# The opening loads of a gated attention and feed-forward kernel: 256-KB second halves, and the Q weights on a second queue

## The chip, the core and the metric

The kernel runs on one core of a Trainium2 chip. A core has five engines that run side by side: TensorE (PE, matrix products, with PEld its weight loads), VectorE (DVE), ScalarE (ACT), GpSimd (POOL) and SyncE (SP). Data come from memory by DMA. A DMA is issued by an instruction on one of the engines' own streams, here SyncE's or ScalarE's, and the transfers of both streams are carried by the same 16 DMA engines. A semaphore tells the waiting engine that a load has landed. The metric is device time in microseconds (us), as the median of several runs.

## What is computed

Cut to what matters, with x of 2048 tokens by 512 in bfloat16:

```python
g = sigmoid((x * gate_w).sum(-1, keepdims=True))
q, k, v = x @ wq, x @ wk, x @ wv            # 32 heads of 16, 4 segments of 512 tokens
for s in range(4):                           # per head
    p = softmax(qs @ ks.T / 4 + causal_mask)
    a_dot = p @ vs
    a_mem = (phi(qs) @ M) / (phi(qs) @ z + 1e-6)
    o_s = sigmoid(beta) * a_mem + (1 - sigmoid(beta)) * a_dot
    M, z = M + phi(ks).T @ vs, z + phi(ks).sum()
a = concat(o_s) @ wo
b = (gelu(x @ w_gate) * (x @ w_up)) @ w_down # inner width 1792
out = g * a + (1 - g) * b
```

## The kernel before

All of the program is a set of named tasks, each a few instructions on one engine. The order in which every engine works through its tasks is written out by hand in the table `ORDER`, one list for each engine, and the streams are emitted in that order. A planner in the file (`Sched`) only merges the five lists into one sequence by estimated times, from which waits between engines are derived; the estimates (`est`, `issue`, the byte counts given to a load) don't reach the chip.

The four segments of 512 tokens are worked through one after the other, each with projections K, Q and V, attention, gate and up products and the down product, interleaved on TensorE. The change lies in the first 10 us or so, the opening.

In the opening, the first segment of x (512 tokens by 512, 512 KB) is loaded in four pieces `x0_0` to `x0_3` of 128 tokens (128 KB each) into `xin`, which is the first part of the buffer `hT[1]`. Pieces 0 and 1 are its first half, pieces 2 and 3 its second. TensorE turns them with 16 transposes (line 596, tasks `x0t0_0`, `x0t1_0` for the first half, `x0t0_1`, `x0t1_1` for the second) into PSUM, and four copies (line 604, tasks `x0ev0_0` to `x0ev1_1`, all on VectorE before) bring the result to `xT[0]`: `x0ev0_1` brings the first 256 input features of the second half's tokens, `x0ev1_1` the other 256. The K weights `wk` come in four blocks of 128 input rows, `w_wk0` to `w_wk3`, of 128 KB each. Before these loads land, seven matmuls on constants keep TensorE busy (line 588, `warm0` to `warm6`).

TensorE's order in the opening is: six `warm` matmuls, transposes of the first half, `warm6`, eight K matmuls on the first half with the first two blocks of `wk`, transposes of the second half, the remaining K matmuls (three of them come later), then Q (blocks 0 and 1 of `wq` are one load, blocks 2 and 3 the other), then V with `wv`. K matmuls in the opening take 256 tokens each, so a name such as `K0_1.6` is segment 0, output tile 1, instruction 6: second half of the tokens, input block 2. Matmuls of all projections carry line 498, copies from PSUM lines 512 (ScalarE) and 515 (VectorE).

All loads are issued by `dma` (line 529; the transposing loads of the later x segments at line 525). SyncE issues, in this order: `x0_0`, `w_wk0`, `x0_2`, `w_wk2`, both halves of `wq`, both halves of `wv` (256 KB each), the first half of the gate weights `wg` (896 KB), the four transposing loads of the second segment of x with the gate vector `gwb` and `beta` between them, and the second half of `wg`. ScalarE issues `x0_1`, `w_wk1`, `x0_3` and `w_wk3`; then it loads the table for exp (`tload`, line 560) and next copies from PSUM.

Of the kernel before, what the change touches and what calls it, by code (L numbers as in the profile page):

```python
# [7 lines left out]
PE, ACT, DVE, POOL, SP = "pe", "act", "dve", "pool", "sp"  # L8
# [13 lines left out]
P = 128  # L22
# [62 lines left out]
        "D3_3w0.4 D3_2.8 D3_2.10 D3_2.12 D3_2.14 D3_3w1.0 D3_3w1.4 D3_3w1.8 D3_0.16 D3_1.14 D3_3w1.12 D3_3a1.0 "  # L85
        "D3_2.16 D3_3w0.8 D3_1.16 D3_3w0.12 D3_3a0.0 "),
    "act": (
        "x0_1 w_wk1 x0_3 w_wk3 tload K0_0even pke0_0 Q0_2ev Q0_1ev Q0_3ev kl0_20 Q0_0ev Vev0_1 K0_3ev exp0_0A0 "
        "gsum0_0 Gev0_6 exp0_0B0 pke0_1 gexp exp0_0L gsum0_3 Gev1_7 exp0_0A1 Q1_0ev exp0_0B1 pqe1_0 gexs0 "
        "exp0_1A0 Gev1_10 Gev1_2 exp0_1B0 pqe1_1 exp0_1A1 K1_0ev Gev0_11 exp0_1B1 gsum1_1 K1_3ev exp0_2A0 Gev1_4 "  # L90
        "exp0_2B0 gsum1_3 Gev0_2 exp0_2L Gev0_7 gexs1 exp0_2A1 Gev1_9 exp0_2B1 Vev1_2 exp0_3A0 Q2_2ev Vev1_3 "
        "exp0_3B0 Gev1_13 Gev0_13 exp0_3A1 Vev1_0 Gev1_1 exp0_3B1 gelu0_0 gelu0_2 Q2_0ev gelu0_6 gelu0_10 "
        "gelu1_0 gelu1_7 exp1_0A0 pke1_0 exp1_0B0 exp1_0L pke1_1 exp1_0A1 fin0_2 exp1_0B1 pqe2_0 exp1_1A0 fin0_0 "
        "exp1_1B0 pqe2_1 exp1_1A1 exp1_1B1 exp1_2A0 exp1_2B0 fin0_3 exp1_2L Vev2_0 exp1_2A1 gsum2_1 exp1_2B1 "
        "exp1_3A0 Q3_0ev exp1_3B0 gexs2 exp1_3A1 Q3_1ev exp1_3B1 gelu2_0 gelu2_1 gelu2_2 gelu2_3 gelu2_4 gelu2_5 "
        "gelu2_6 gelu2_7 gelu2_8 gelu2_9 gelu2_10 gelu2_11 gelu2_12 gelu2_13 exp2_0A0 pke2_0 exp2_0B0 pke2_1 "
        "exp2_0L Q3_3ev Vev3_0 exp2_0A1 exp2_0B1 pqe3_0 exp2_1A0 exp2_1B0 pqe3_1 exp2_1A1 exp2_1B1 K3_0ev "
        "exp2_2A0 exp2_2B0 exp2_2L exp2_2A1 exp2_2B1 exp2_3A0 gsum3_2 exp2_3B0 exp2_3A1 K3_3ev exp2_3B1 gexs3 "
        "gelu3_0 gelu3_1 gelu3_2 gelu3_3 gelu3_4 gelu3_5 gelu3_6 gelu3_7 gelu3_8 gelu3_9 gelu3_10 gelu3_11 "
        "gelu3_12 gelu3_13 exp3_0A0 exp3_0B0 exp3_0L exp3_0A1 fin2_0 exp3_0B1 exp3_1A0 exp3_1B0 exp3_1A1 "  # L100
        "exp3_1B1 exp3_2A0 exp3_2B0 exp3_2L exp3_2A1 exp3_2B1 exp3_3A0 exp3_3B0 exp3_3A1 exp3_3B1 fin3_0 fin3_1 "
        "fin3_30 "),
    "dve": (
        "x0ev0_0 x0ev1_0 x0ev0_1 x0ev1_1 K0_1ev kl0_11 K0_0ev kp0_1 kl0_01 kl0_10 K0_2ev kp0_2 kl0_21 gmul0 "
        "kp0_0 kl0_00 Vev0_0 pkc0_0 Vev0_2 kp0_3 Gev0_1 Q1_2ev Gev1_5 Gev0_4 kl0_30 kl0_31 Vev0_3 pkc0_1 Q1_3ev "
        "gsum0_2 Gev1_11 Q1_1ev gsum0_1 Gev0_8 K1_2ev pqc1_0 Gev1_3 gmat Gev0_5 mzacc0 pvt0_0_0 pvt0_0_1 pqc1_1 "
        "gmul1 Gev1_12 K1_1ev gsum1_0 Gev0_12 Gev0_10 GdT0 Vev1_1 norm0_0 pvt0_1_0 pvt0_1_1 mzbd0 Gev0_9 gsum1_2 "
        "Gev1_6 gts1 Gev1_8 nump1_00 Gev0_3 nump1_01 nump1_02 norm0_1 Q2_1ev pvt0_2_0 pvt0_2_1 kp1_0 nump1_11 "
        "norm0_2 Gev0_0 pvt0_3_0 nump1_10 Q2_3ev Gev1_0 pvt0_3_1 Um0_0 Um0_1 norm0_3 Um0_2 Um0_9 Um0_7 Um0_8 "
        "Um0_12 Um0_4 Um0_6 Um1_2 Um0_3 Um1_3 Um1_5 Um0_5 kl1_00 Um0_13 kl1_01 Um0_11 nump1_12 kp1_1 Um0_10 "  # L110
# [17 lines left out]
        "msk2_3B1 msk2_3A0 msk2_3B0 exsT3 msk3_0B0 msk3_0A0 msk3_0L msk3_0A1 msk3_0B1 msk3_1A1 msk3_1B1 msk3_1A0 "  # L128
        "msk3_1B0 msk3_2B0 msk3_2L msk3_2A1 msk3_2A0 msk3_2B1 msk3_3A0 msk3_3B0 msk3_3A1 msk3_3B1 "),
    "sp": (  # L130
        "x0_0 w_wk0 x0_2 w_wk2 w_wq0 w_wq1 w_wv0 w_wv1 w_wg0 x1_0 w_gwb x1_1 w_beta x1_2 x1_3 w_wg1 pkT0_1 "
        "Vlo0_0 Vlo0_1 pkT0_2 pkT0_0 pkT0_3 xt1 x2_3 x2_2 x2_1 x2_0 w_wu0 oTd1_1 oTd1_0 w_wu1 w_wd1 w_wo Vlo1_1 "
        "w_wd0 x3_2 Vlo1_0 oTd1_2 pkT1_0 x3_0 oTd1_3 pkT1_3 x3_1 pkT1_2 pkT1_1 x3_3 xt2 out0 Vlo2_1 oTd2_0 out3 "
        "out1 oTd2_1 pkT2_1 out4 Vlo2_0 pkT2_2 pkT2_3 pkT2_0 out2 oTd2_3 oTd2_2 xt3 out7 oTd3_0 Vlo3_0 oTd3_1 "
        "out8 Vlo3_1 out11 oTd3_3 out6 oTd3_2 out5 out9 out10 out12 out15_1 out14 out13 out15_0 "),
}
GAP = {DVE: 0.012, POOL: 0.063}
HOP = {PE: 0.25, ACT: 0.07, DVE: 0.07, POOL: 0.10, SP: 0.0}
# [284 lines left out]
def _build(es, nc, A_x, A_wq, A_wk, A_wv, A_wo, A_beta, B_w_gate, B_w_up, B_w_down, gate_w, out):  # L423
    def sb(name, shape, dtype=BF):
        return es.enter_context(nc.sbuf_tensor(name, shape, dtype))
# [17 lines left out]
    hT = [sb(f"hT{i}", [P, NFT, 512]) for i in range(2)]  # L443
# [11 lines left out]
    gexp = sb("gexp", [P, H], F32)  # L455
    gtmp = sb("gtmp", [P, H], F32)
    gmat = sb("gmat", [P, H], F32)
# [11 lines left out]
    wq = sb("wq", [P, 4, 512])  # L469
    wk = sb("wk", [P, 4, 512])  # L470
    wv = sb("wv", [P, 4, 512])
# [8 lines left out]
    for i in range(N_W):  # L480
        w = es.enter_context(nc.psum_tensor(f"psW{i}", [P, 512], F32))
# [6 lines left out]
    def sem(name):  # L488
        nsem[0] += 1
        return es.enter_context(nc.semaphore(f"{name}_{nsem[0]}"))  # L490
# [3 lines left out]
    def task(name, eng, instrs, **kw):  # L494
        return S.add(Task(name, {eng: instrs}, **kw))

    def mm(g, view, lhsT, rhs, reads, first, last, n, fkey=None):
        return Instr(lambda e: e.matmul(view(), lhsT, rhs, start=first, stop=last),  # L498
                     reads=reads, writes=[fkey if fkey is not None else g.key], est=mm_t(n))

    def pieces(name, g, instrs, size, after=(), bias=0.0):

        r = None
        for i in range(0, len(instrs), size):
            r = task(f"{name}.{i}", PE, instrs[i:i + size], grp=g, after=after, bias=bias)
        return r
# [12 lines left out]
    def dma(name, eng, out_ap, in_ap, reads, writes, nbytes, issue=0.5, transpose=False, bias=0.0, sm=None,  # L519
            nonc=False, after=()):  # L520
        sm = sm if sm is not None else sem("d")

        def f(e):
            if transpose:
                return e.dma_start_transpose(out_ap(), in_ap())
            if nonc:
                with nc.allow_non_contiguous_dma(reason="small vector"):
                    return e.dma_start(out_ap(), in_ap())
            return e.dma_start(out_ap(), in_ap())
        return task(name, eng, [Instr(f, reads, writes, issue, dma_sem=sm)], bias=bias, nbytes=nbytes, after=after)  # L530

    rank = [1.0e6]
# [5 lines left out]
    def wdma(key, eng, dst, src, nbytes, nonc=False, issue=0.5, reads=()):  # L538
        rank[0] -= 20000.0 if rank[0] > 1.0e5 else 20.0
        dma("w_" + str(key), eng, lambda: dst, lambda: src, list(reads), [("w", key)], nbytes, bias=rank[0],  # L540
            nonc=nonc, issue=issue)
# [8 lines left out]
    r4 = lambda w: w.rearrange("(kb p) n -> p kb n", p=P)  # L550
# [9 lines left out]
    task("tload", ACT, [Instr(lambda e: e.activation(stmp[:, 0:1], ones[:, 0:1], ACTF.Exp), writes=[("stmp",)],  # L560
                              est=1.5)], bias=1.0e5)
    xin = hT[1][:, 0:4, :]
    def x0dma(a):
        rank[0] -= 20000.0
        dma(f"x0_{a}", (SP, ACT)[a % 2], lambda: xin[:, a, :], lambda: A_x[0, a * 128:(a + 1) * 128, :], [],
            [("hT", 1, a)], 140000, bias=rank[0], issue=0.45)

    x0dma(0)
    x0dma(1)
    for kb in range(4):  # L570
        wdma(("wk", kb), (SP, ACT)[kb % 2], wk[:, kb, :], A_wk[128 * kb:128 * kb + 128, :], 170000, issue=0.45)
    x0dma(2)
    x0dma(3)
    for key, w, src in (("wq", wq, A_wq), ("wv", wv, A_wv)):
        for i in range(2):
            wdma((key, i), SP, w[:, 2 * i:2 * i + 2, :], r4(src)[:, 2 * i:2 * i + 2, :], 250000)
    wdma(("wg", 0), SP, wg[:, :, 0:half], wgr[:, :, 0:half], 790000)
    xdma(1, 0, 2)
    wdma("gwb", SP, gwb[:], gate_w.partition_broadcast(P), 115000)
# [5 lines left out]
    for i in range(7):  # L585
        gw = Grp(banks)
        n = 512 if i < 6 else 384
# [4 lines left out]
    for u in range(2):  # L592
        for i in range(2):
            src = XB[:, 1024 * (2 * u + i):1024 * (2 * u + i) + 512].rearrange("p (k c) -> p k c", c=256)
            key = ("X", 2 * u + i)
# [11 lines left out]
    for g in range(4):  # L607
# [8 lines left out]
         bias=3000.0)  # L616
# [46 lines left out]
    def proj_T(name, s, t, w, wkey, dst, wkeys, even=None):  # L663

        head = s == 0
        x = head and wkey == "wq"
        g = None if x else Grp(banks)
        view = (lambda: X[t]) if x else (lambda: g.f32()[:, :])
        key = ("X", t) if x else g.key
        xs = xT[s % NX]  # L670
        nu = 2 if head and wkey == "wk" else 1
        cols = [slice(512 // nu * u, 512 // nu * (u + 1)) for u in range(nu)]
        wk_of = lambda kb: ("w", (wkey, kb if wkey == "wk" else kb // 2))
        pieces(name, g, [mm(g, lambda c=c: view()[:, c], w[:, kb, t * 128:(t + 1) * 128], xs[:, kb, c],
                            [*(xk(s, kb)[u:u + 1] if nu > 1 else xk(s, kb)), wk_of(kb)],
                            kb == 0, kb == 3, 512 // nu, fkey=key)
                         for u, c in enumerate(cols) for kb in range(4)], 1 if nu == 2 else 2)
        if even is not None:
            task(name + "even", ACT, [Instr(lambda e: e.activation(even[0], view(), ACTF.Copy,
                                                                   scale=maskc[0][:, 0:1]),  # L680
                                            [key, ("c", "mask", 0)], [even[1]], act_t(512, ap=True))], grp=g)
        copy_out(name + "ev", g, lambda: dst[:, t, :], view, [key], wkeys, 512)
# [501 lines left out]
```

## Time and profile before

| | |
|---|---|
| median of 7 runs | 268.39 us (268.18 to 270.14) |
| the profiled execution | 270.14 us, span 268.4 us, granted clock 0.998 |
| TensorE busy | 256.5 us, 96% |
| ScalarE busy | 209.4 us, 78% |
| VectorE busy | 198.9 us, 74% |
| GpSimd busy | 105.1 us, 39% |
| DMA | 18.23 MB, mean 68 GB/s |
| DMA from SyncE's queue (q1) / ScalarE's (q10) | 17.25 MB / 0.52 MB |

The profiled execution is the one with the longest time of the seven. The profile's times count from the start of its span. A group row gives a line of the kernel, an engine, an operation and the tile that it writes and reads (the program's names without buffer numbers, so `hT` stands for `xin` too), then the time. `SPq` and `ACTq` are the instruction streams of SyncE and ScalarE where they issue a DMA. "Landing" is the time from the issue of a load until its semaphore is complete. The chain of waits follows the work that ended last back to the start. In the windows, the share of DMA is the mean busy share of the 16 DMA engines and may exceed one where packets overlap.

### The profile page before, as it was taken

What the parts mean: (1) busy time and instruction counts of PE and PEld (TensorE: products, weight loads), DVE (VectorE), ACT (ScalarE), POOL (GpSimd) and SP (SyncE); (2) the same over time, 40 slices, a digit from 0 to 9 for tenths busy, and PEclk for the clock granted to TensorE, in tenths of its full rate; (3) what the DMA queues carried; (4) which work ended last, traced back from release to release, by engine and by line L of the source; (5) the groups of instructions that cost most, each with busy time, mean ns of one, the idle gap of its engine ahead of it and who ended that gap; (6) DMA issues with size and microseconds to landing.
All of it is one profiled execution on the core that took longest, in us unless ns stands there. A gap on an engine that the chain in (4) does not pass through costs nothing.

```text
span 268.4 us, 7104 instructions
## 1 busy us (share of the span) xinstructions
PE 256.5 (96%) x2976; PEld 119.2 (44%) x3017; DVE 198.9 (74%) x390; ACT 209.4 (78%) x185; POOL 105.1 (39%) x256
## 2 busy tenths in 40 slices
PE   6999999999999999999999999999999999999994
PEld 2744444445444444444444444443444444343452
DVE  1598888988888588895768968898685847693641
ACT  2399998999999898898867888867876887776702
POOL 8102768463101257173830162354173061436210
PEclk9999999999999999999999999999999999999999
DMA  5971422517530343200001333200000031300002
GB/s 178 336 187 23 87 81 57 163 22 247 174 112 0 82 78 66 97 0 2 2 0 21 98 83 78 82 4 20 4 2 0 2 81 42 78 4 22 22 0 81
DMA packets 32816, 18.23 MB, mean 68 GB/s; under 512 B 20624, under 2 KB 32784, under 8 KB 32784
## 3 DMA queue, kind: packets, MB, share of 16 engines
q1 hardware_dynamic: 32208, 17.25, 24.0%
q8 instruction: 24, 0.39, 0.6%
q10 hardware_dynamic: 576, 0.52, 0.6%
q14 instruction: 8, 0.07, 0.1%
HBM read 9.84 MB, written 2.10 MB: 44 GB/s over the span
## 4 chain that ended last, share of the span: by engine, by line
PE 89%; ACT 3%; DVE 3%; issue 2%; DMA 2%; ACTq 0%
PE psW L498 69%; PE psXALL L864 9%; PE psW L914 6%; PE psXALL L498 3%; ACT pt L871 2%; DMA hT<-in_A_x_dram 2%; PE psW L922 1%; PE psW L830 1%; PE psXALL L596 1%; DVE tb L929 0%; ACT L998 0%; DVE phkt L753 0%; ACT hT L998 0%; DVE glog L761 0%; DVE klow L712 0%
## 5 line engine op out<-in xcount | busy, mean ns | idle before, releaser
L871 ACT ACTIVATE pt<-psXALL 128x2048 bf16<-128x2048 f32 x64 | 120.1, 1877 | 25.4 <-PE psXALL L864 20.3
L875 POOL TENSOR_SCALAR_AFFINE_SELECT pt<-pt 128x256 bf16<-128x256 bf16 x128 | 57.9, 461 | 107.0 <-ACT pt L871 102.4
L498 PE MATMUL psW<-xT,wu 128*128 128x512 bf16 x218 | 55.1, 380 | 0.8 <-issue 0.6
L498 PE MATMUL psW<-xT,wg 128*128 128x512 bf16 x212 | 51.5, 379 | 1.6 <-issue 1.0
L498 PE MATMUL psW<-wd,hT 128*128 128x512 bf16 x198 | 51.1, 379 | 1.6 <-issue 1.4
L1014 DVE TENSOR_TENSOR hT<-psW,hT 128x512 bf16<-128x512 f32 x56 | 37.2, 685 | 18.5 <-PE psW L498 18.2
L875 POOL TENSOR_SCALAR_AFFINE_SELECT ptl<-ptl 128x512 bf16<-128x512 bf16 x32 | 23.0, 718 | 34.9 <-ACT ptl L871 33.3
L929 DVE STREAM_TRANSPOSE tb<-psW 128x512 f32<-128x512 f32 x32 | 21.5, 699 | 14.0 <-PE psW L922 13.9
L498 PEld LDWEIGHTS psW<-xT,wg 128*128 128x128 bf16 x224 | 20.4, 98 | 24.3 <-issue 1.5
L498 PEld LDWEIGHTS psW<-xT,wu 128*128 128x128 bf16 x224 | 20.2, 98 | 24.4 <-issue 2.7
L498 PEld LDWEIGHTS psW<-wd,hT 128*128 128x128 bf16 x210 | 19.2, 98 | 22.8 <-issue 2.1
L864 PE MATMUL psXALL<-qT,kpad 32*128 32x320 bf16 (+3 forms) x512 | 25.4, 273 | 0.5 <-ACT pt L871 0.2
L998 ACT ACTIVATE hT<-psW 128x512 bf16<-128x512 f32 x28 | 15.4, 600 | 8.0 <-PE psW L498 8.0
L864 PEld LDWEIGHTS psXALL<-qT,kpad 32*128 32x128 bf16 x512 | 7.6, 92 | 26.0 <-ACT pt L871 16.3
L914 PE MATMUL psW<-pt,vaug 128*17 128x192 bf16 (+3 forms) x512 | 18.8, 273 | 0.0
L498 PE MATMUL psW<-xT,wk 128*128 128x512 bf16 (+1 forms) x79 | 18.4, 350 | 0.2 <-issue 0.2
L871 ACT ACTIVATE ptl<-psXALL 128x2048 bf16<-128x2048 f32 x8 | 15.0, 1877 | 3.7 <-PE psXALL L864 3.7
L498 PE MATMUL psW<-wv,xT 128*128 128x512 bf16 x60 | 16.4, 380 | 0.5 <-DVE glog L761 0.2
L498 PE MATMUL psW<-wo,oT 128*128 128x512 bf16 x57 | 15.7, 379 | 0.5 <-issue 0.2
L773 POOL COPY exsT<-exs 32x4 f32<-32x4 f32 x64 | 13.4, 209 | 7.2 <-ACT exs L764 3.5
L914 PEld LDWEIGHTS psW<-pt,vaug 128*17 128x17 bf16 x512 | 10.3, 90 | 8.8 <-issue 3.0
L515 DVE CAST hT<-psW 128x512 bf16<-128x512 f32 x16 | 10.9, 684 | 2.8 <-PE psW L498 2.4
(100 smaller groups left out, 308.2 us busy)
## 6 DMA issues: line engine op xcount, KB each, us to landing
out_dram<-ost SPq DMA_DIRECT2D x15, 128.0 KB, 1.7
wg<-in_B_w_gate_dram SPq DMA_DIRECT2D x2, 896.0 KB, 6.9
wu<-in_B_w_up_dram SPq DMA_DIRECT2D x2, 896.0 KB, 5.1
wd<-in_B_w_down_dram SPq DMA_DIRECT2D x2, 896.0 KB, 5.8
phkt<-in_A_x_dram SPq DMA_DIRECT2D x3, 512.0 KB, 3.7
vlow<-vaug SPq DMA_DIRECT2D x8, 136.0 KB, 2.7
wq<-in_A_wq_dram SPq DMA_DIRECT2D x2, 256.0 KB, 5.3
wv<-in_A_wv_dram SPq DMA_DIRECT2D x2, 256.0 KB, 5.7
```

Of the source, the lines that this page charges most:

```text
L498: return Instr(lambda e: e.matmul(view(), lhsT, rhs, start=first, stop=last), reads=reads, writes=[fkey if fkey is not None else g.key], e ...
L515: alts[DVE] = [Instr(lambda e: e.tensor_copy(dst(), src()), reads=reads, writes=writes, est=dve_t(n))]
L596: task(f"x0t{i}_{u}", PE, [Instr(lambda e, k=k, a=a, u=u, i=i, src=src: e.transpose(src[:, k, a * 128:(a + 1) * 128], xin[:, 2 * u + a, (2 ...
L773: cross = task(f"exsT{s}", POOL, [Instr(lambda e, g=g, c=c: e.tensor_copy(exsT[sl][32 * g:32 * g + 32, c:16:4], exs[32 * c:32 * c + 32, s4 ...
L830: Instr(lambda e, t=t, kt=kt, c=c: e.matmul(gm.f32()[32 * c:32 * c + 32, 34 * t:34 * t + 34].rearrange("p (j e) -> p j e", e=17), phkt[:, ...
L864: instrs.append(Instr(lambda e, g=g, lhs=lhs, rhs=rhs, c0=c0, ncol=ncol: e.matmul(X[g][:, c0:c0 + ncol], lhs(32 * g), rhs(32 * g), start=T ...
L871: prev_exp[0] = exp_task(s, f"exp{s}_{t}{name}", [Instr(lambda e: e.activation(dst[:], XALL[:, :].rearrange("p (g c) -> p g c", g=4), ACTF ...
L875: task(f"msk{s}_{t}{name}", POOL, [Instr(lambda e, view=view, pat=pat, base=base: e.affine_select(out=view, in_=view, compare_op=ALU.is_ge ...
L914: instrs.append(Instr(lambda e, t=t, q=q, kb=kb, slot=slot, c0=c0: e.matmul(gp.f32()[32 * q:32 * q + 17, 128 * kb + 64:512], Vaug[sl][:, k ...
L929: task(f"pvt{s}_{t}_{j}", DVE, [Instr(lambda e: e.transpose(Tb[:, j, :], gp.f32()[:, :]), [gp.key], [("Tb", j)], dve_t(512))], grp=gp)
L998: lambda e, g=g, ft=ft, s=s: e.activation(hT[s % 2][:, ft, :], g.f32()[:, :], ACTF.Gelu_apprx_tanh),
L1014: task(f"Um{s}_{ft}", DVE, [Instr(lambda e, g=g, ft=ft: e.tensor_tensor(hT[sl][:, ft, :], g.f32()[:, :], hT[sl][:, ft, :], ALU.mult), [g.k ...
```

## The change

The second halves of x0 and wk become one load of 256 KB each: `x0_2` now brings tokens 256 to 511 and is issued by ScalarE as its third load; `w_wk2` brings input blocks 2 and 3 and is issued by SyncE as its third. `x0_3` and `w_wk3` are gone. The first halves stay as they were. Both halves of `wq` move from SyncE's stream to ScalarE's, after `x0_2`; `wv` stays on SyncE and follows `w_wk2`. The copy `x0ev1_1` moves from VectorE to ScalarE, after `tload`. The readers of wk blocks 2 and 3 wait for the one load. TensorE's and GpSimd's orders are unchanged, and so are all lists beyond the opening.

```diff
     "act": (
-        "x0_1 w_wk1 x0_3 w_wk3 tload K0_0even pke0_0 ...
+        "x0_1 w_wk1 x0_2 w_wq0 w_wq1 tload x0ev1_1 K0_0even pke0_0 ...
     "dve": (
-        "x0ev0_0 x0ev1_0 x0ev0_1 x0ev1_1 K0_1ev kl0_11 ...
+        "x0ev0_0 x0ev1_0 x0ev0_1 K0_1ev kl0_11 ...
     "sp": (
-        "x0_0 w_wk0 x0_2 w_wk2 w_wq0 w_wq1 w_wv0 w_wv1 w_wg0 x1_0 w_gwb ...
+        "x0_0 w_wk0 w_wk2 w_wv0 w_wv1 w_wg0 x1_0 w_gwb ...
...
-    def x0dma(a):
+    def x0dma(u, e, a0, n):
         rank[0] -= 20000.0
-        dma(f"x0_{a}", (SP, ACT)[a % 2], lambda: xin[:, a, :], lambda: A_x[0, a * 128:(a + 1) * 128, :], [],
-            [("hT", 1, a)], 140000, bias=rank[0], issue=0.45)
-
-    x0dma(0)
-    x0dma(1)
-    for kb in range(4):
-        wdma(("wk", kb), (SP, ACT)[kb % 2], wk[:, kb, :], A_wk[128 * kb:128 * kb + 128, :], 170000, issue=0.45)
-    x0dma(2)
-    x0dma(3)
-    for key, w, src in (("wq", wq, A_wq), ("wv", wv, A_wv)):
+        dma(f"x0_{u}", e, lambda: xin[:, a0:a0 + n, :],
+            lambda: A_x[0, a0 * 128:(a0 + n) * 128, :].rearrange("(a p) d -> p a d", p=P), [],
+            [("hT", 1, a0 + a) for a in range(n)], 145000 * n, bias=rank[0], issue=0.45)
+
+    def wkdma(u, e, k0, n):
+        wdma(("wk", u), e, wk[:, k0:k0 + n, :], r4(A_wk)[:, k0:k0 + n, :], 150000 * n, issue=0.45)
+
+    x0dma(0, SP, 0, 1)
+    x0dma(1, ACT, 1, 1)
+    wkdma(0, SP, 0, 1)
+    wkdma(1, ACT, 1, 1)
+    wkdma(2, SP, 2, 2)
+    x0dma(2, ACT, 2, 2)
+    for key, w, src, e in (("wq", wq, A_wq, ACT), ("wv", wv, A_wv, SP)):
         for i in range(2):
-            wdma((key, i), SP, w[:, 2 * i:2 * i + 2, :], r4(src)[:, 2 * i:2 * i + 2, :], 250000)
+            wdma((key, i), e, w[:, 2 * i:2 * i + 2, :], r4(src)[:, 2 * i:2 * i + 2, :], 250000, issue=0.46)
...
-        wk_of = lambda kb: ("w", (wkey, kb if wkey == "wk" else kb // 2))
+        wk_of = lambda kb: ("w", (wkey, min(kb, 2) if wkey == "wk" else kb // 2))
```

## The prediction

> **What bounds the kernel now.** I read first the page's busy times and its chain of work, to see which engine sets the end:
>
> ```profile
> PE 256.5 (96%) x2976; PEld 119.2 (44%) x3017; DVE 198.9 (74%) x390; ACT 209.4 (78%) x185; POOL 105.1 (39%) x256
> ...
> PE 89%; ACT 3%; DVE 3%; issue 2%; DMA 2%; ACTq 0%
> ```
>
> TensorE (PE) is busy 96% of the span and is 89% of the chain; DMA is 2% of it. The change touches only the first loads, so next I read the chain in order of time for the first microseconds (start, length, what):
>
> ```profile
> 0.81 4.13 DMA hT<-in_A_x_dram
> 4.93 0.05 issue
> 4.98 1.10 PE psXALL L596 x8
> 6.07 0.32 PE psW L588
> 6.39 1.60 PE psW L498 x8
> 7.99 0.45 PE psXALL L596 x8
> 8.44 2.29 PE psW L498 x21
> ```
>
> All the DMA on this path is the first x0 load, issued at 0.81 and landed at 4.93. From 4.98 on TensorE works without a break: transposes of the first half (L596), a warm-up matmul, eight K matmuls, transposes of the second half, 21 more K matmuls, then Q. No later load is on the chain. The question is therefore when each load is needed, against when it lands. Needs, from the timeline (start, length):
>
> ```profile
> 7.68 0.58 PEld L596 LDWEIGHTS psXALL<-ident,hT 128*128 128x128 bf16 x8
> 8.25 0.76 DVE L604 COPY xT<-psXALL 128x512 bf16<-128x512 bf16 x2 [1.72 <-PE psXALL L596]
> 10.46 1.93 PEld L498 LDWEIGHTS psXALL<-xT,wq 128*128 128x128 bf16 x10
> 14.35 1.89 PE L498 MATMUL psW<-wv,xT 128*128 128x512 bf16 x8
> ```
>
> The second half of x0 is needed at 7.68, the second half of wk at 8.22 (the next weight loads), wq at 10.46, wv at 14.35. Landings, from the DMA issues cut down to single issues (last column: us from issue to landing):
>
> ```profile
> hT<-in_A_x_dram SPq DMA_DIRECT2D x1, 128.0 KB, 4.5
> hT<-in_A_x_dram ACTq DMA_DIRECT2D x1, 128.0 KB, 4.6
> ...
> wk<-in_A_wk_dram SPq DMA_DIRECT2D x1, 128.0 KB, 4.6
> wk<-in_A_wk_dram ACTq DMA_DIRECT2D x1, 128.0 KB, 4.9
> ...
> wq<-in_A_wq_dram SPq DMA_DIRECT2D x1, 256.0 KB, 5.1
> ...
> wq<-in_A_wq_dram SPq DMA_DIRECT2D x1, 256.0 KB, 5.6
> ```
>
> Added to their issue times: x0 second half 1.72 + 4.5 = 6.2 and 1.73 + 4.6 = 6.3; wk second half 2.19 + 4.6 = 6.8 and 2.21 + 4.9 = 7.1; wq 2.66 + 5.1 = 7.8 and about 3.15 + 5.6 = 8.7. Everything is there 1.1 to 2.7 us before it is wanted.
>
> **The change, part by part.** The profiled execution took 270.14 us with a span of 268.4, the highest of the seven; the median is 268.39. I add differences to the median.
>
> *First halves (x0_0, x0_1, wk0, wk1).* They keep their size, queue and place, so the landing at 4.93 that starts the chain stays: 0.
>
> *Second half of x0, now 256 KB on ScalarE's queue.* It keeps its issue at 1.73. The nearest row for 256 KB is wq: 5.1, at most 5.6. It lands at 6.8 to 7.3; if the second 128 KB cost nothing, at 1.73 + 4.5 = 6.2. I take 6.8, since the first wq load is also 256 KB and close in time. Needed at 7.68: nothing is lost in this execution.
>
> *Second half of wk, now 256 KB on SyncE's queue at about 1.72.* Same rows: 6.2 to 7.3, against 8.22. Half a microsecond earlier issued, about as early landed as before: 0.
>
> *wq to ScalarE's queue, beside wv.* These two windows (us, busy time of PE, PEld, DVE, ACT and POOL, granted clock, DMA share, GB/s) set its bounds:
>
> ```profile
> 4.00:6.00 2.00, 1.02 (x9) 0.87 (x9) 0.32 (x1) 0.19 (x1) 2.00 (x2) 1.00 0.85 278
> 6.00:8.00 2.00, 2.00 (x14) 1.36 (x13) 0.53 (x2) 0.00 (x0) 2.00 (x3) 1.00 1.07 369
> ```
>
> From 4 to 6 both queues deliver (45% and 41% of the time of the 16 engines) and together make 278 GB/s; from 6 to 8 SyncE's queue has nearly all (95%) and makes 369. By 6.0 about 0.93 MB has moved (2 us at 180, 2 us at 278 and a little before). x0, wk, wq and wv are 2.10 MB, so 1.17 MB is left: 3.2 us at 369, 4.2 us at 278, ending at 9.2 to 10.2. A load lands some 0.6 later (the last wk packets on ScalarE's queue went out at about 6.5 and the load landed at 7.1). So wq's second load, which used to land at 8.7, lands at 9.8 to 10.8. It is first read by the third pair of Q matmuls, 4 x 0.216 after 10.57, at 11.43. Its first load has half a megabyte less ahead of it, 8.4 to 8.9, against 10.46. wv: up to 10.8 against 14.35. Later than before, and still covered: 0. Cover left: 0.6 us at the worst.
>
> [...]
>
> *What moves up on SyncE's queue.* It loses x0_2 (1.72 to 2.19, 0.47 us) and the two wq issues (2.66 to 3.65, 0.99 us): 1.46 us. So wg0 is issued at about 3.5 instead of 4.95, and the x1 transposes, gwb, beta and wg1 behind it also up to 1.46 earlier. Were any of them late? wg0 landed at 4.95 + 7.5 = 12.5 (needed 16.94), x1's first two pieces at 13.0 and 14.0 (needed 16.50), gwb at 7.55 + 5.8 = 13.4 (needed by VectorE at 14.56), wg1 at 13.09 + 6.4 = 19.5 (needed 22.57). None was, so a head start earns 0; the bytes ahead of them are the same, so none turns late.
>
> *ScalarE.* Five issues of about 0.47 instead of four: the exp table load starts at 3.15 instead of 2.69 and, with 1.28 + 0.20, ends at 4.65. Then comes the moved copy x0ev1_1. The last transpose ends at 8.22 + 0.22 = 8.44; a ScalarE copy of 512 columns takes 0.59 (L512) to 0.69 (L679): done at 9.03 to 9.13. On VectorE it was done at 8.25 + 0.76 = 9.01. Its first reader is the tenth K matmul after 8.276, at 8.276 + 9 x 0.109 = 9.26; a matmul followed a copy by 0.09 at 6.19. So 9.12 to 9.22 against 9.26: 0, with 0.04 to 0.14 to spare. Behind it on ScalarE stands only the K copy at 10.18; VectorE, relieved of 0.42, then waits for K anyway (0.67 idle before 9.68): 0.
>
> Sum: 0, so 268.4 us. Its own range is 268.1 to 268.8: down 0.26 (TensorE's idle time between 4.98 and 30: windows over the first 30 us give it 27.48 busy, and 0.84 and 1.42 of the rest lie before 4.98), up 0.4 for the covers that follow.
>
> **How thin the covers can get.** TensorE ran at half rate until 7.8: K matmuls of 256 columns stood 0.213 apart before and 0.109 after, though the granted clock in both windows reads 1.00. In an execution that is at full rate from 4.98, the second copy wait and eight K matmuls come sooner: the second half of x0 is wanted about 1.0 us earlier (7 x 0.104, plus 0.2 to 0.3 on the transposes before them), at 6.7. Then 6.8 costs 0.1 and 7.3 costs 0.6; the second load of wq, wanted at 10.4, would cost up to 0.4, not on top, since a wait at 6.7 moves the later need. That is where +0.4 comes from.
>
> [...]
>
> **Rivals.**
>
> *Slower: the second half of x0 becomes the wait.* One load now carries it, sharing the engines with the equally large wk load, and signals nothing until all 256 KB are in. It decides from a landing after 7.68, that is 5.95 us after issue. Against: no 256-KB row above 5.7 (wv's median). For: wg0 took 7.5, as the farthest row; it is 896 KB and would put the landing at 9.2, a loss of 1.5. About halfway between the two points the loss is 0.9 us (a landing at 8.6): 269.3.
>
> *Faster: the opening shortens by more than its idle time.* Idle time gives 0.26 at most, so this needs TensorE at full rate sooner: from 4.98 on it is worth 1.0 us, 267.4. For: the half-rate stretch is real. Against: nothing TensorE does before 7.68 is changed.
>
> *The change doesn't do what it says:* the larger loads run at 278 GB/s like the small ones. Then the late end of every landing above holds: still covered, 268.4 to 268.8. It is part of the forecast's range.
>
> **How the numbers follow.** Differences under 0.3% (0.8 us) are about what a measurement of this kernel can't tell from no change. Forecast, covered loads: 0.64. Slower rival: 0.22, as the covers are thin at full rate. Faster rival: 0.14. The time is the forecast's, 268.4. The range leaves out the far halves of both rivals: 267.6 to 269.4.
>
> **What would show it.** Right: the chain still starts with the first x0 load at 4.9, no DMA wait of TensorE after it, second half of x0 landing at 6.2 to 7.3, wq's second load before 11.4, wg1 about a microsecond earlier with no one gaining. Wrong: a TensorE wait on hT, wk or wq between 6.7 and 11.4, a wait on ScalarE's copy at about 9.3, a first landing that is not 4.9, or a K spacing that changes from 0.213 to 0.109 at another time.

## The result, and the profile after

The changed kernel takes 269.82 us (median of 27 runs, 267.97 to 271.86) against 268.19 us for the kernel before (64 runs, 267.36 to 270.14). The ratio is 1.0061 with a 95% interval of 1.0046 to 1.0076: slower by 0.6%, some 1.6 us. The forecast was no change, and the median lies above its range.

The chain of the changed kernel in order of time (start, length, what):

```profile
0.80 0.40 ACTq L529
1.20 0.03 issue
1.23 0.46 ACTq L529
1.70 0.03 issue
1.73 5.98 DMA hT<-in_A_x_dram
7.71 0.05 issue
7.75 0.62 PE psXALL L600 x8
8.37 2.29 PE psW L498 x21
```

The chain no longer goes through the first x0 load. It goes through the issues on ScalarE's queue and the third of them, x0's second half, which takes 5.98 us to land. TensorE's timeline (start, length, idle time before and what ended it):

```profile
3.47 1.09 PE L600 MATMUL psXALL<-ident,hT 128*128 128x128 bf16 x8
4.67 1.59 PE L498 MATMUL psW<-xT,wk 128*128 128x256 bf16 x8
7.75 0.62 PE L600 MATMUL psXALL<-ident,hT 128*128 128x128 bf16 x8 [1.49 <-DMA hT<-in_A_x_dram]
```

The first transposes start at 3.47, 1.5 us sooner than in the profile before, and the K matmuls are through at 6.3. Then TensorE stands idle until x0's second half is there. The DMA issues of the opening, each from a stretch with that issue in it (KB, us to landing):

```profile
hT<-in_A_x_dram ACTq DMA_DIRECT2D x1, 128.0 KB, 2.8
hT<-in_A_x_dram SPq DMA_DIRECT2D x1, 128.0 KB, 2.6
...
wk<-in_A_wk_dram SPq DMA_DIRECT2D x1, 256.0 KB, 5.3
hT<-in_A_x_dram ACTq DMA_DIRECT2D x1, 256.0 KB, 6.0
...
wq<-in_A_wq_dram ACTq DMA_DIRECT2D x1, 256.0 KB, 8.1
```

A puzzle stands here: the changed kernel's profiled span, 267.3 us, is shorter than the 268.4 us before, though its median is longer. The profile before was of an unusually late execution: no other of the 64 runs took longer than its 270.14 us. A second and a third profile of that kernel, taken among the experiments, have spans of 266.0 and 265.7 us. TensorE in the third:

```profile
3.69 0.76 PE L596 MATMUL psXALL<-ident,hT 128*128 128x128 bf16 x8
4.74 1.05 PE L498 MATMUL psW<-xT,wk 128*128 128x256 bf16 x8
5.63 0.61 PE L596 MATMUL psXALL<-ident,hT 128*128 128x128 bf16 x8
6.10 2.76 PE L498 MATMUL psW<-xT,wk 128*128 128x256 bf16 x21
8.92 2.11 PE L498 MATMUL psXALL<-xT,wq 128*128 128x512 bf16 x9
```

Here x0's first half lands at 3.6, and the second transposes follow the K matmuls at 5.63 without a wait. The first transposes take 0.76 us, against 1.10 in the first profile, at half rate, and 0.61 for the second ones here: by these lengths TensorE reaches full rate at about 4.0 (an estimate). What the opening loses stays lost to the end:

| execution | first Q matmul recorded | span |
|---|---|---|
| before, first profile | 10.78 | 268.4 |
| before, second | 9.19 | 266.0 |
| before, third | 8.92 | 265.7 |
| changed, first | 10.72 | 267.3 |
| changed, second | 10.57 | 267.1 |
| changed but wq on SyncE's queue | 12.30 | 269.0 |

From the second row on, the span is the time of the first Q matmul and 256.5 to 256.8 us; in the first row it is 0.8 us more, and where that went isn't shown. The times run about 1.75 us above the spans, so the kernel's median of 268.19 stands for a first Q matmul at about 9.8 (an estimate from these rows): the second and third profiles, of 267.74 and 267.52 us, are of executions somewhat faster than the median one.

### The profile page after: what moved, and what is told of

Same layout as the page of the kernel before. It is cut to its first block, busy times and chain, and to the rows that moved or that the text cites. A ratio compares the mean times of both kernels' runs of the same rounds, so it can differ in the third digit from the quotient of the medians.

```text
span 267.3 us, 7102 instructions
## 1 busy us (share of the span) xinstructions
PE 256.3 (96%) x2976; PEld 119.1 (45%) x3017; DVE 198.1 (74%) x389; ACT 210.0 (79%) x186; POOL 105.2 (39%) x256
## 3 DMA queue, kind: packets, MB, share of 16 engines
q10 hardware_dynamic: 1104, 1.05, 1.2%
## 4 chain that ended last, share of the span: by engine, by line
PE 89%; DVE 3%; ACT 3%; DMA 2%; issue 2%; ACTq 0%
PE psW L498 69%; PE psXALL L868 9%; PE psW L918 6%; PE psXALL L498 3%; DMA hT<-in_A_x_dram 2%; ACT pt L875 1%; PE psW L926 1%; PE psW L834 1%; DVE tb L933 1%; ACT L1002 0%; DVE phkt L757 0%; ACT hT L1002 0%; DVE glog L765 0%; ACTq L529 0%; DVE klow L716 0%
## 5 line engine op out<-in xcount | busy, mean ns | idle before, releaser
L879 POOL TENSOR_SCALAR_AFFINE_SELECT pt<-pt 128x256 bf16<-128x256 bf16 x128 | 57.0, 454 | 106.6 <-ACT pt L875 101.9
L991 ACT ACTIVATE hT<-hT 128x2048 bf16<-128x2048 bf16 (+2 forms) x6 | 12.7, 2185 | 0.0
```

Of the source, the lines that this page charges most:

```text
L879: task(f"msk{s}_{t}{name}", POOL, [Instr(lambda e, view=view, pat=pat, base=base: e.affine_select(out=view, in_=view, compare_op=ALU.is_ge ...
L991: t = task(f"gelu{s}_{f0}", ACT, [Instr(lambda e, hv=hv: e.activation(hv, hv, ACTF.Gelu_apprx_tanh), hk, hk, act_t(512 * n, False) + (-0.1 ...
```

## The experiments

Theory 1 says that x0's second half comes late because its one 256-KB load shares the DMA engines with an equally large wk load, where the two 128-KB pieces before went ahead of wk on both queues. Theory 2 blames wq on ScalarE's queue and the loads that move up on SyncE's; theory 3 the copy that moved to ScalarE. Ratios are against runs of the kernel before on the same chip. The edits are cut to what matters; the lists in `ORDER` were changed to match.

**The kernel before, again.**

> The kernel before, unchanged, for a second profile of it: the first one had its first x0 load land at 4.9 us, the changed kernel's at 3.4. If that difference is one of single executions, this profile shows a first landing near 3.4 to 4.9, a second half of x0 that lands by 6.4 and hardly a wait of TensorE for it, and the ratio is 1.000. If the first landing belongs to the kernel, it is 4.9 again.

268.24 us, ratio 0.9995 (0.9972 to 1.0018). First x0 piece at 0.81 + 2.8 = 3.6, second half 3.9 and 4.1 us after issue, at 5.6 and 5.8. So the first landing at 4.9 belonged to that one execution.

**The kernel before, a third profile.**

> The kernel before, unchanged, for a third profile: how often its x0 halves land at 4.9 and 6.3, as in the first, and how often at 3.6 and 5.7, as in the second. Theory 1 needs the second half by 6.4 in either case.

One execution, 267.52 us. x0's second half took 3.2 and 3.3 us, so the three profiles of this kernel have it at 6.3, 5.8 and 5.0.

**x0's second half in two loads again.**

```diff
 # of the changed kernel
+    x0dma(2, SP, 2, 1)
+    x0dma(3, ACT, 3, 1)
     wkdma(2, SP, 2, 2)
-    x0dma(2, ACT, 2, 2)
```

> The changed kernel, with only x0's second half back in two 128-KB loads, one on each queue ahead of wk's second half. Theory 1 (the half shares the engines with an equally large wk load instead of going ahead of it in both queues, so 1.0 MB instead of 0.75 MB has to move before it lands): it lands by 6.4, TensorE waits for it under 0.5 us, ratio 0.997 to 1.001. Theory 2 (wq on ScalarE's queue and the earlier wg and x1 loads crowd the opening): still late, ratio 1.004 or more. Theory 3 (the copy moved to ScalarE): ratio 1.004 or more, with an idle TensorE after the second transposes.

268.97 us, ratio 1.0026 (1.0009 to 1.0044): under half of the loss first measured, and by its interval mostly outside the range theory 1 had named. TensorE:

```profile
4.77 1.87 PE L498 MATMUL psW<-xT,wk 128*128 128x256 bf16 x8
6.65 0.75 PE L601 MATMUL psXALL<-ident,hT 128*128 128x128 bf16 x8
8.35 0.82 PE L498 MATMUL psW<-xT,wk 128*128 128x256 bf16 x6 [0.96 <-DMA wk<-in_A_wk_dram]
```

This execution shows no wait for x0, but that is partly luck. The two pieces took 4.9 and 5.1 us and landed at 6.6 and 6.8, later than the 6.4 that theory 1 had named. TensorE was at half rate, so its first K matmuls took 1.87 us and ended at 6.64; with the 1.05 us of the profiles at full rate they would have ended at 5.8, and the same landings would have cost about 0.8 us (an estimate). And there is another wait: wk's 256-KB half, now behind x0's piece and beside wq on the other queue, lands 6.0 us after its issue at 2.19, at 8.2.

**wq back on SyncE's queue.**

```diff
 # of the changed kernel
-    for key, w, src, e in (("wq", wq, A_wq, ACT), ("wv", wv, A_wv, SP)):
+    for key, w, src, e in (("wq", wq, A_wq, SP), ("wv", wv, A_wv, SP)):
```

> The changed kernel, with only wq back on SyncE's queue ahead of wv. Theory 1: x0's second half still lands at 7 us or later and the ratio stays at 1.004 to 1.007. Theory 2: it lands by 6.5 and the ratio is 0.997 to 1.001. Theory 3: 1.004 or more.

270.0 us, ratio 1.0054 (1.0015 to 1.0092). x0's second half still takes 6.0 us. TensorE's busy time, granted clock and DMA in windows:

```profile
5.00:6.00 1.00, 0.81 (x8) 1.00 0.84 220
6.00:7.00 1.00, 0.00 (x0) 1.00 0.88 290
7.00:8.00 1.00, 0.21 (x3) 0.80 1.03 351
8.00:9.00 1.00, 1.00 (x10) 0.50 1.08 375
9.00:10.00 1.00, 1.00 (x7) 0.50 1.07 399
10.00:11.00 1.00, 1.00 (x7) 0.50 1.06 410
11.00:12.00 1.00, 1.00 (x11) 0.99 1.76 288
```

The wait costs twice here. TensorE is idle for 2.0 us, and in the midst of it the granted clock (the number after the count in brackets) falls to 0.50 and stays there from 7.6 to 11.0: matmuls of 256 columns stand 0.213 apart in place of 0.109. Five of the ten executions show a mean clock of 0.994, with 270.8 to 272.3 us; the other five have a median of 268.98. Theory 2 falls.

**wq alone moved.** The kernel before, with `wq` issued by ScalarE behind `w_wk3`.

> The kernel before, with only wq moved to ScalarE's queue, behind its 128-KB loads. Theory 1: x0's second half lands by 6.4 as before, wq's second load at 9 to 11, no wait, ratio 0.998 to 1.001. Theory 2: x0's second half lands later than 6.8, ratio 1.003 or more. Theory 3: 1.000.

268.38 us, ratio 1.0003 (0.9982 to 1.0024). x0's half took 3.5 and 3.9 us. wq did become late, with two waits of 0.6 us together, which the expectation had not allowed for. In this profile the V matmuls start at 13.69, against 12.75 and 12.48 in the second and third of the kernel before, yet the median of ten doesn't show it; the interval reaches to 0.24%, so 0.6 us is at its very edge.

**x0's second half alone in one load.**

```diff
 # of the kernel before
-    x0dma(2)
-    x0dma(3)
+    rank[0] -= 20000.0
+    dma("x0_2", ACT, lambda: xin[:, 2:4, :], lambda: A_x[0, 256:512, :].rearrange("(a p) d -> p a d", p=P), [],
+        [("hT", 1, 2), ("hT", 1, 3)], 290000, bias=rank[0], issue=0.45)
```

> The kernel before, with only x0's second half as one 256-KB load on ScalarE's queue; wk's second half stays two 128-KB loads, and wq stays on SyncE's queue. Theory 1: SyncE's queue goes straight on with wk and wq, so the half still shares with as many bytes: it lands 5.5 to 6.2 us after its issue instead of 4.0, TensorE waits 1 to 2 us for it, ratio 1.003 to 1.007. Rival (only the pair of 256-KB loads is slow, wk's merging being what hurts): it lands within 4.6 us, ratio 0.999 to 1.001.

269.14 us, ratio 1.0043 (1.0014 to 1.0073). The half lands 5.7 us after its issue:

```profile
4.57 1.75 PE L498 MATMUL psW<-xT,wk 128*128 128x256 bf16 x8
7.51 0.62 PE L597 MATMUL psXALL<-ident,hT 128*128 128x128 bf16 x8 [1.19 <-DMA hT<-in_A_x_dram]
```

This one part brings most of the loss by itself. wk's second half was two loads of 128 KB here, so theory 1 asks for too much: what shares the engines needn't be one equally large wk load.

**wk's second half alone in one load, twice.** The kernel before, with `w_wk2` of 256 KB on SyncE's queue behind `x0_2`, and `w_wk3` gone.

> The kernel before, with only wk's second half as one 256-KB load on SyncE's queue, behind x0_2; x0's second half stays two 128-KB loads on both queues. Theory 1: x0's half lands early (within 4.5 us of its issue), wk's half lands 5 to 6 us after its issue at 2.2 instead of 4.4, TensorE waits 0.5 to 1.2 us for it, ratio 1.001 to 1.004. Rival (x0's merging alone hurts): wk's half lands by 6.9, ratio 1.000.

> The kernel before, with only wk's second half as one 256-KB load behind x0_2, once more, since its first profile showed waits of 1.2 us and its times no loss. If the waits are typical the ratio is 1.001 to 1.004; if that profile was one of late loads, the waits are under 0.6 us and the ratio is 0.999 to 1.001.

268.18 us, ratio 1.0003 (0.9981 to 1.0024), and 268.48 us, ratio 1.0011 (0.9994 to 1.0028). The half landed 5.3 and 5.0 us after its issue, and TensorE waited 0.42 and 0.88 us for it (in the first also 0.78 for x0). A loss of 0.1% is possible, but not shown: neither expectation is clearly met.

**x0's second half with SyncE's queue held back.**

```diff
 # of the changed kernel
-    wkdma(2, SP, 2, 2)
+    wkdma(2, SP, 2, 2, [("hT", 1, 0)])       # waits for the first x0 piece
...
```

> The changed kernel, with SyncE's issue of wk's second half (and all behind it) held until the first x0 piece has landed, so that x0's 256-KB second half has the engines nearly to itself after the first halves. The times are not of interest, wk now comes late (about 8.5) and TensorE waits for that. Theory 1 (the bytes that share the engines set the landing): x0's second half lands 3.5 to 4.6 us after its issue. Rival (one 256-KB load is slow to be complete by itself, whatever runs beside it): 5.5 us or more.

Its issues, and TensorE:

```profile
hT<-in_A_x_dram ACTq DMA_DIRECT2D x1, 256.0 KB, 4.2
...
wk<-in_A_wk_dram SPq DMA_DIRECT2D x1, 256.0 KB, 5.8
```

```profile
6.02 0.62 PE L600 MATMUL psXALL<-ident,hT 128*128 128x128 bf16 x8
9.37 0.81 PE L498 MATMUL psW<-xT,wk 128*128 128x256 bf16 x6 [2.73 <-DMA wk<-in_A_wk_dram]
```

The same load that took 5.8 and 6.0 us in the changed kernel takes 4.2 in this one profile, with SyncE's loads held back to 3.43, and the second transposes follow without a wait; wq still runs behind it on its own queue. wk then comes late, as foreseen (269.82 us, ratio 1.0075, 1.0028 to 1.0123). So its size alone doesn't make it late; what the other queue sends beside it does.

**The idle time filled.**

```diff
 # of the changed kernel, ahead of x0t0_1 on TensorE
+    for i in range(7):
+        task(f"fill{i}", PE, [Instr(lambda e: e.matmul(X[0], ones[:, 0:128], ones[:, 0:512], start=True, stop=True),
+                                    [], [("X", 0)], mm_t(512))])
```

> The changed kernel, with seven more matmuls on constants (1.5 us at full rate, their result unused) between the eight first K matmuls and the transposes of x0's second half. If part of the loss is TensorE's rate, dropping to half for a while after the idle wait in some executions, then no execution shows a mean granted clock of 0.994, the slow group of 270.4 to 271.9 is gone and the ratio is 1.002 to 1.005. If the loss is the wait alone, the spread stays and the ratio is 1.006 or more.

269.28 us, ratio 1.0042 (1.0026 to 1.0059), highest 270.05.

```profile
5.69 1.69 PE L611 MATMUL psXALL<-const-bfloat16-1.0 128*128 128x512 bf16 x7
8.05 0.62 PE L600 MATMUL psXALL<-ident,hT 128*128 128x128 bf16 x8 [0.67 <-DMA hT<-in_A_x_dram]
```

None of its ten executions shows a mean granted clock under 0.997. So, in ten executions, matmuls that compute nothing of use make the changed kernel's tail disappear: 269.28 is also the median of those executions in its first measurement whose clock didn't fall. In the median they gain nothing over the changed kernel measured again, below, which has 1.0035 without them.

**The changed kernel, again.**

> The changed kernel, unchanged, beside the others on one chip, for a second profile and a count of the executions with a mean granted clock of 0.994. Theory 1: x0's half lands 5.7 to 6.3 us after its issue, a third to a half of the executions show 0.994 and are about 2 us longer than its others, ratio 1.004 to 1.008.

268.94 us, ratio 1.0035 (1.0010 to 1.0060). x0's half took 5.8 us, TensorE waited 1.75. Three of twelve executions show a clock of 0.986 to 0.994, with 271.3 to 272.7 us; the other nine have a median of 268.82. In the first measurement ten of 28 (the profiled one included) had 0.992 to 0.994, with a median of 271.0 us, and the other 18 one of 269.28. The loss is less here: fewer executions lost the clock, and those that kept it took less time too, 268.82 against 269.28, for which no cause is shown. One of ten lost it with x0's half alone merged, and one of six with SyncE's queue held back. Of 89 executions of the kernel before in these comparisons none is under 0.997.

**Everything but the two large loads.** The kernel before, with `wq` on ScalarE's queue and the copy `x0ev1_1` on ScalarE.

> The kernel before, with the two parts of the change that load nothing larger: wq on ScalarE's queue and the copy x0ev1_1 on ScalarE; both second halves stay two 128-KB loads each, one on each queue. Theory 1: x0's half lands within 4.6 us of its issue, no execution at a granted clock of 0.994, ratio 0.998 to 1.002. Theories 2 and 3: ratio 1.003 or more, and for theory 3 an idle TensorE at the tenth matmul after the second transposes.

268.22 us, ratio 0.9996 (0.9979 to 1.0012). x0's half took 3.8 and 4.2 us; nothing waited for the copy, and wq was waited for twice:

```profile
9.75 0.81 PE L498 MATMUL psXALL<-xT,wq 128*128 128x512 bf16 x3 [0.24 <-DMA wq<-in_A_wq_dram]
10.93 0.82 PE L498 MATMUL psXALL<-xT,wq 128*128 128x512 bf16 x3 [0.37 <-DMA wq<-in_A_wq_dram]
```

Theories 2 and 3 fall with it: without the two 256-KB halves the rest of the change costs nothing that shows (at most 0.12% by the interval). No experiment points to a version that beats the kernel before.

## Why the prediction was wrong

**What bounds the kernel.** Right that TensorE sets the end. Wrong that no later load is on the path: that was read from one execution, in which the first x0 load landed at 4.93 and TensorE was at half rate until 7.8. In the other two profiles of the same kernel the second transposes start at 5.63, not at 7.83. Every "needed at" of the prediction was 1.6 to 2.2 us too late for these two executions, and by the estimate above about one too late for the median one.

**x0's second half, the step that failed.** "I take 6.8, since the first wq load is also 256 KB and close in time", against a need at 7.68. It landed at 7.7 and 7.6, and TensorE was through with its earlier work at 6.3 and 5.9. Both terms of the comparison failed: by the prediction's own need of 7.68 a landing at 7.7 would still have cost nothing. The row for the landing was ill chosen: from 6 to 8, while wq's first load came to its end, SyncE's queue had 95% of the engines' time, whereas the changed half runs beside wk's equally large load and what follows it on SyncE's queue. With SyncE's queue held back it takes 4.2 us, beside other large loads 5.7 to 6.3 (five profiles). The prediction did its byte count for wq, where it was right (9.8 to 10.8, measured about 10.8 and 10.5), and not for x0. The same count for x0, 1.05 MB to move instead of 0.79, at the 282 GB/s of the changed kernel's window from 4 to 6, gives 0.9 us. The measured difference is larger, 5.7 to 6.3 against 3.2 to 4.6 in the kernel before. The traces show the rest as bytes too: by the time x0's half was whole, both queues together had moved 1.53 to 1.70 MB in those five profiles, and 0.86 to 1.07 MB in the three of the kernel before. Against the count of 1.05 and 0.79, in the changed kernel 0.5 to 0.65 MB of loads issued later had gone ahead of the large half, in the kernel before 0.07 to 0.28 MB. Why more goes ahead of it isn't settled.

**The slower rival** (0.22) had the mechanism and the place: one load, sharing the engines, waited for by TensorE. That its 269.3 came near is partly luck: it took a landing of 8.6 against 7.68, and both came sooner, 7.6 to 7.7 against 5.9 to 6.3. The paragraph on thin covers saw the need move to 6.7 in an execution at full rate, and counted up to 0.6 for it; it moves to about 5.7, and the wait is 1.2 to 2.0.

**What was missing** is the second price of the wait. Some executions lose the clock, for 3.4 us in the one that was profiled, and take longer: by their medians 1.7 us in the first measurement (271.0 against 269.28), 2.4 with wq back and 2.8 in the changed kernel measured again. The median of 269.82 lies between the two groups, which overlap: two of the 18 that kept the clock took 270.82 and 271.78 us, and no profile shows why.

**wk's second half** was expected covered. Alone it costs little (0.42 and 0.88 us of waits, ratios 1.0003 and 1.0011). With wq beside it the loss was 0.3%, in a run whose x0 pieces were late as well.

**wq on ScalarE's queue: 0,** right in the sum, and the landing was right (10.8, and 10.5 in the second profile). Its cover was not: 0.6 us of waits with wq moved alone and 0.6 with the copy moved too, which the medians, 1.0003 and 0.9996, don't show.

**What moves up on SyncE's queue: 0,** right, but not by the way described. wg0 was issued at 3.21 in place of 4.95 and gwb at 6.10 in place of 7.55, while wg1 came at 13.16 against 13.09: the x1 transposes took longer to issue (2.18, 2.46 and 3.26 us for the last two together, before 2.04, 1.17 and 3.03), so the head start was used up on the way. "wg1 about a microsecond earlier" was wrong.

**The copy on ScalarE: 0,** right: done at 8.41 + 0.60 = 9.01, forecast 9.03 to 9.13, and no wait followed.

## What to carry to other kernels

In an opening that waits for loads, look at all the bytes that both queues send, not at the count of loads: here x0's 256-KB load took 5.7 to 6.3 us to land beside the other queue's large loads, and 4.2 in the one profile with that queue held back. Cutting a half that must come first over both queues, ahead of what can wait, helped here but doesn't make it sure: with a 256-KB wk load behind them the two x0 pieces took 4.7 to 5.1 us in two of three runs, against 3.2 to 4.2 in the four profiles without such a load, the late first one aside. A time of need read from one profile is only as good as that execution; look at the spread of the runs, and if the profiled one is at its edge, shift every need before calling a load covered. A wait of TensorE cost its clock as well in some executions here, five of ten with wq back (mean clock 0.994, and 2.4 us by the medians), so price both.

## What the runs showed of the hardware

In the run with wq back on SyncE's queue TensorE was idle from 5.80 to 7.79, and its granted clock read 1.00 from 4 to 7.6, 0.50 to 11.0 and 1.00 to 13: 3.4 us at half. The length of the gap doesn't order the profiles: the clock fell in one of 2.0 us there, and in none of 1.5 and 1.75 us in the changed kernel's two profiles, nor in the one of 2.7 us with SyncE's queue held back (mean clock 1.000 in all three). What decides whether a given wait costs the clock isn't shown.

When TensorE came to its full rate differed between the executions too: the first eight K matmuls took 1.03 to 1.05 us in nine of the fourteen profiles, and 1.59 to 1.92 in the other five.

The first 128-KB load on SyncE's queue landed 2.5 to 2.8 us after its issue in thirteen of the fourteen profiles, and 4.1 in the other, the first of the kernel before.
